# A polysketch attention with an FFN behind it: the order of its instructions from a table of priorities, more PSUM banks for the first FFN product, and batch 1's kv kept on chip

## The chip, the cores and the metric

The kernel runs on one core of a Trainium2 chip. The metric is device time in microseconds (us), the median of the runs; lower is better. One core has TensorE (PE: matmuls; PEld: the loading of their weights), VectorE (DVE), ScalarE (ACT), GpSimd (POOL) and SyncE (SP, which only issues DMAs here). Each engine works through its own list of instructions in order, and waits on semaphores for the others.

## The reference

```python
def _attn_ref(q, k, v, S1, S2):              # 4 batches, 4 heads, 1088 tokens, 32 wide
    ...
    def phi(x):
        a = np.einsum('rd,bhsd->bhsr', S1, x)    # r = 8
        b = np.einsum('rd,bhsd->bhsr', S2, x)
        return np.einsum('bhsi,bhsj->bhsij', a, b).reshape(*x.shape[:-1], r * r)
    q_p, k_p = (phi(q), phi(k))
    kv = np.einsum('bhsf,bhsd->bhfd', k_p, v)
    z = np.sum(k_p, axis=2)
    num = np.einsum('bhsf,bhfd->bhsd', q_p, kv)
    den = np.einsum('bhsf,bhf->bhs', q_p, z)[..., None] + 1e-06
    return (num / den).astype(np.float32)

def _moe_ref(x, w_in, w_out):                # 4352 x 128, 128 x 2048, 2048 x 128
    h = x @ w_in
    g = h - np.tanh(h)
    return (g @ w_out).astype(np.float32)
```

The attention's result, its heads side by side, is the FFN's x.

## The kernel before, in words

**Attention, batch by batch.** For each of the four batches k is loaded and transposed by DVE (tile kT, L602), sketched by PE (L620, "ksk"), transposed back (abk, L634, "kab"), and its outer products are formed on DVE (w, L680, three pieces); PE multiplies them with v into kv (L692). A small gram product (L652, L643) with two ACT copies (gm, L661; sc, L668) gives the denominator's weights. kv then has to be brought into the form that the numerator reads, the tile kvb (`kv_tail`, L716). For batch 0 this is done on chip: a copy kvd (L728), two PE transposes (L735), a copy kvb (L738). For batches 1 to 3 DVE transposes into kvd (L719), SP stores it to a scratch tensor kvx in memory (L721, called kvs) and loads it four times from there into kvb (L723). On q's side DVE transposes (qT, L611), PE sketches (L756, "qsk"), DVE transposes back (abc, L762), divides (m, den, rd, ap: L774 to L782), and forms outer products (qp, L800) and their transposes (qpT, L805), three pairs for a whole batch. PE's numerator (L818, "num") needs kvb and qpT, fills four PSUM banks and is copied to xT in two halves (L390) by ACT or DVE. The next batch's sketch needs those banks, so it waits for the copies.

**FFN, in ten groups of columns.** `GCOLS` (L19) cuts the 4352 token columns into groups of 256, 384, 448, six of 512, and 192. A group has 16 first products, h = w_in's block times xT (L927), 16 tanhs by ACT (th, L931) and 18 second products that add up in one bank (16 with th, L942, and two correction products of xT with w_in w_out, split in two bf16 parts wch and wcl, L946); then DVE transposes the bank (ot, L951) and SP stores it (L961). Groups 0 to 2 are batch 0's columns, 3 and 4 lie in batch 1's, 5 begins there and needs batch 2, 6 lies in batch 2's, and 7 to 9 need batch 3.

**PSUM** has eight banks. Before, the h tiles of groups 0 to 6 turn through banks 0, 1 and 2, one bank to a tanh; the second products use bank 3; attention has banks 4 to 7. From group `PAIRS` = 7 on an h tile takes two banks, (4, 5), (6, 7) or (0, 1), and one tanh reads both; these groups wait for the end of attention (`att_end`).

**The order** is found when the program is built. Every operation is given engines with a planned duration and a delay, a key (lower goes first), its reads and writes, and pools of buffers to choose from. `schedule` (L158) takes at each step, for every engine, the ready operations that could start within a small window (L35) of the earliest, the one with the lowest key among these, and of the engines' choices the earliest; it gives it a free buffer and moves on. So planned durations and keys decide the order on each engine, and which bank an operation gets; nothing is decided at run time. `sync` (L279) then puts in the semaphore waits. Attention's keys count up in program order from -50000 (batch 0's first part -65000); an FFN operation's key is its group's due time plus its number times a step (L915 to L934); loads on SP go first, each held back until an earlier load has landed (`CAPS`, `more`).

Of the kernel before, what the change touches and what calls it, by code (L numbers as in the profile page):

```python
# [12 lines left out]
FP32 = mybir.dt.float32  # L13
# [12 lines left out]
WKEY = (300.0, 300.0, 1500.0)  # L26
PAIRS = 7
URGENT = (-60500.0, 450.0)
# [65 lines left out]
class _Op:  # L94
    __slots__ = ("engs", "fn", "key", "deps", "users", "nleft", "vals", "eng", "lat", "mode",
                 "t0", "t1", "seq", "known", "waits", "inc", "cnt", "sem", "dma", "name", "filler", "parts")


class _Prog:
    SWITCH = 125.0  # L100

    def __init__(self):
        self.ops = []

    def add(self, engs, fn, r=(), w=(), key=0.0, chain=None, dma=0, name="", after=(), mode=None, parts=1):
# [32 lines left out]
        o.deps.pop(o, None)  # L138
        self.ops.append(o)
        return o  # L140

# [219 lines left out]
def bass_polysketch_attn__then__act_tanh_shrink_kernel(  # L361
# [37 lines left out]
    pair_h = _Pool([(pb[i:i + 2], [bank(i, 2)]) for i in (4, 6, 0)], True)  # L399
    att1 = one(4, 5, 6, 7)  # L400
# [106 lines left out]
    def load_k(key, b, more=None):  # L507
        src = k[b].rearrange("h (t r c) d -> (h t) r (c d)", r=2, c=17)
        if b == 0:
            for e in range(2):  # L510
                op = load(key + e, kvals[b][e].ap, src[:, :, e * 288:(544 if e else 288)], [kvals[b][e]], 128 * (256 if e else 288) * 8, issue=750.0, more=more, wire=950.0 - 80 * e)
            return op
        return load(key, kL[b][:, :], k[b].rearrange("h (t c) d -> (h t) (c d)", c=NC), kvals[b] + (kvals[0] if b == 3 else []), 128 * 1088 * 4, cap=2, more=more, wire=1450.0)

    def load_v(key, b, more=None):
        ops = []
        vs = v[b].rearrange("h (m x) d -> m h (x d)", x=17)
        for e in range(2):
            w_ = 256 if e else 288
            ops.append(load(key + e, vL[b][e * 64:(e + 1) * 64, :, 0:w_], vs[:, :, e * 288:e * 288 + w_], [vvals[b][e]] + (vvals[0] if b == 3 else []), 64 * w_ * 16, cap=1 + (b > 0), issue=630.0, more=more, wire=1150.0 - 80 * e))  # L520
        return ops

    def load_q(key, b, i, more=None):
        a, z, val = qvals[b][i]
        src = q[b].rearrange("h (t c) d -> (h t) (c d)", c=NC)
        return load(key, qL[b][:, a * 32:z * 32], src[:, a * 32:z * 32], [val] + ([x[2] for x in qvals[0]] if b == 3 else []), 128 * (z - a) * 128, cap=1 + (b > 0), more=more, wire=(z - a) * 43.0 + 100)

# [59 lines left out]
    def nk():  # L587
        seq[0] += 1
        return -50000.0 + seq[0] + bias[0]
# [80 lines left out]
    wvs = {}  # L670
    kvx = [nc.dram_tensor(f"kvx{i}", [128, 64], FP32, kind="Internal").ap() for i in range(3)]

# [43 lines left out]
    def kv_tail(b):  # L716
        kvd, kvb = _Val(kvd_p), kvbv[b]
        if b:
            P.add(_vp(64), lambda e, n: e.transpose(kvd.ap[:, 0:64], pv[b].ap[:, 0:64]), r=[pv[b]], w=[kvd], key=nk(), name=f"kvd{b}")  # L719
            kvs = _Val()  # L720
            P.add({"sync": (450.0, 0.0)}, lambda e, n: e.dma_start(out=kvx[b - 1], in_=kvd.ap[:, 0:64]), r=[kvd], w=[kvs], key=nk(),  # L721
                  dma=-2300.0, name=f"kvs{b}")
            P.add({"sync": (450.0 * 4, 0.0)}, lambda e, n: [e.dma_start(  # L723
                out=kvb.ap[g * 32:(g + 1) * 32, :, :, :].rearrange("p h x d -> p h (x d)"),
                in_=kvx[b - 1].rearrange("(h f) y -> f h y", h=4)) for g in range(4)],
                r=[kvs], w=[kvb], key=nk(), dma=-3800.0, parts=4, name=f"kvb{b}")
            return
# [60 lines left out]
    def q_piece(b, s0, b0, b1, abc, aq):  # L788
# [24 lines left out]
        def num(e, n):  # L813
# [76 lines left out]
    def weights():  # L890
        for i in range(2):
            tp = _Val(one(4 + 2 * i))
            for j in range(8):
# [20 lines left out]
    def ffn(gi, c0, n_):  # L914
# [8 lines left out]
        for jb in range(NJB):  # L923
            if jb % m == 0:
                hv, th = _Val(pair_h if late else bank_h), _Val(th2_p if late else th_p)
            ths.append((th, jb % m))
            P.add(_pe(n_ / 2.4 + 2.6), lambda e, n, jb=jb, hv=hv: e.matmul(  # L927
                hv.ap[:, jb % m * 512:jb % m * 512 + n_], wic(jb), xt, start=True, stop=True),
                r=[wi[jb // 8]] + xs, w=[hv], key=-60000.0 if gi == 0 and jb < 3 else t0 + jb * step, mode="128x128", name=f"h{gi}.{jb}", after=att_end if late else ())
            if jb % m == m - 1:  # L930
# [110 lines left out]
```

## Time and profile before

| | |
|---|---|
| runs (us) | 112.22, 114.05, 113.49; median 113.49 |
| the profiled execution's own time | 114.35 us |
| its span, first to last instruction | 112.3 us, so 2.05 us lie around it |
| mean granted PE clock | 0.985 of full speed |
| busy: PE, PEld, DVE, ACT, POOL | 99.8, 54.1, 68.3, 78.4, 4.9 us |
| HBM | 9.21 MB read, 2.33 MB written |

A line of the time line reads: start in us, duration in us, engine, source line, operation, output <- input, shapes, how many instructions in a row are merged into it, and in brackets how long the engine sat idle before and for whom. A line of the waits reads: engine, line, whom it waited for, us in total, times, longest. SPq is SP issuing DMAs. The page's part 2 cuts the span into 40 slices of 2.8 us; each digit is the busy share in tenths, PEclk the granted clock in tenths.

### The profile page before, as it was taken

Reading aid. Unit: us, or ns where it says so; the run is one execution under the profiler, and the core shown is the slowest. Engines: PE = TensorE matmul, PEld = TensorE weight load, DVE = VectorE, ACT = ScalarE, POOL = GpSimd, SP = SyncE. Lnnn points to the kernel's source line nnn. Section 1 sums busy time; section 2 is a strip of 40 time slices with the busy share of each in tenths; the row PEclk is TensorE's granted clock in tenths of the full one; section 3 lists DMA queues with packets and bytes.
Section 4 is the critical chain, followed back from the end, with each engine's and each line's share of the span. In section 5 each row is a group of like instructions: output and inputs, shape, how many; then the busy total and the mean of one; then the engine's idle time right before and its main releaser. Section 6 shows DMA issues by size and latency. Waiting matters only on the chain.

```text
span 112.3 us, 3312 instructions
## 1 busy us (share of the span) xinstructions
PE 99.8 (89%) x1421; PEld 54.1 (48%) x1430; DVE 68.3 (61%) x107; ACT 78.4 (70%) x160; POOL 4.9 (4%) x25
## 2 busy tenths in 40 slices
PE   5899969999999927999999999999999999999920
PEld 6746736564564503244633344644444455455800
DVE  4469769999999990099999699998220020200210
ACT  2100747788669851395698687689799999999910
POOL 5250300000000000000000000000000000000000
PEclk9999999999999998599999999999999999999999
DMA  1999798154762397535803400025003214014071
GB/s 19 261 221 198 162 181 317 38 126 90 212 155 88 75 205 166 124 147 85 206 17 67 68 1 0 18 43 97 6 3 58 33 20 73 6 23 70 0 107 24
DMA packets 25087, 10.70 MB, mean 95 GB/s; under 512 B 20977, under 2 KB 23665, under 8 KB 25073
## 3 DMA queue, kind: packets, MB, share of 16 engines
q1 hardware_dynamic: 23792, 9.36, 36.9%
q0 software_dynamic: 576, 1.05, 5.8%
q8 instruction: 11, 0.18, 0.7%
q10 hardware_dynamic: 704, 0.08, 0.5%
q14 instruction: 4, 0.02, 0.1%
HBM read 9.21 MB, written 2.33 MB: 103 GB/s over the span
## 4 chain that ended last, share of the span: by engine, by line
PE 35%; DMA 24%; DVE 15%; ACT 13%; SPq 5%; issue 2%; DVEq 0%
ACT th L931 13%; PE psb L942 13%; PE psb L927 11%; DMA qL<-in_q_dram 9%; DMA vL<-in_v_dram 9%; PE psb L818 5%; SPq L494 4%; DMA kL<-in_k_dram 4%; DVE qp L800 3%; DMA kvb<-kvx 3%; DVE w L680 2%; DVE abc L762 2%; PE psb L620 2%; DVE ot L951 1%; PE psb L692 1%
## 5 line engine op out<-in xcount | busy, mean ns | idle before, releaser
L931 ACT ACTIVATE th<-psb 128x512 bf16<-128x512 f32 (+4 forms) x136 | 69.7, 631 | 11.3 <-PE psb L927 6.9
L927 PE MATMUL psb<-xT,wi 128*128 128x512 bf16 (+4 forms) x154 | 50.3, 362 | 1.3 <-issue 0.4
L942 PE MATMUL psb<-th,wo 128*128 128x512 bf16 (+4 forms) x157 | 47.4, 353 | 1.1 <-issue 1.0
L927 PEld LDWEIGHTS psb<-xT,wi 128*128 128x128 bf16 x160 | 22.0, 145 | 23.6 <-ACT th L931 12.5
L942 PEld LDWEIGHTS psb<-th,wo 128*128 128x128 bf16 x160 | 15.2, 102 | 12.3 <-ACT th L931 4.3
L951 DVE STREAM_TRANSPOSE ot<-psb 128x512 f32<-128x512 f32 (+4 forms) x10 | 6.3, 627 | 24.0 <-PE psb L942 24.0
L805 DVE STREAM_TRANSPOSE qpT<-qp 128x768 f32<-128x768 f32 (+1 forms) x13 | 11.8, 909 | 0.3
L800 DVE TENSOR_TENSOR qp<-ap,abc 128x768 f32<-128x768 f32 (+1 forms) x13 | 11.2, 864 | 0.1
L680 DVE TENSOR_TENSOR w<-abk 128x768 f32<-128x768 f32 x12 | 10.8, 950 | 0.1
L818 PE MATMUL psb<-qpT,kvb 32*32 32x288 f32 (+3 forms) x384 | 8.0, 338 | 2.6 <-DMA kvb<-kvx 2.6
L390 ACT CAST xT<-psb 128x192 bf16<-128x192 f32 (+4 forms) x10 | 4.3, 472 | 6.3 <-PE psb L818 6.3
L454 PE MATMUL psb<-zz 128*128 128x134 bf16 (+1 forms) x56 | 7.2, 298 | 1.1 <-DVE zz L453 1.1
L634 DVE STREAM_TRANSPOSE abk<-psb 128x288 f32<-128x288 f32 x8 | 3.3, 457 | 6.8 <-PE psb L620 6.8
L818 PEld LDWEIGHTS psb<-qpT,kvb 32*32 32x32 f32 x384 | 4.5, 103 | 5.3 <-DMA kvb<-kvx 2.9
L602 DVE STREAM_TRANSPOSE kT<-kL 128x576 f32<-128x576 f32 (+1 forms) x8 | 5.5, 714 | 1.9 <-DMA kL<-in_k_dram 1.9
L454 PEld LDWEIGHTS psb<-zz 128*128 128x128 bf16 x56 | 5.4, 129 | 2.1 <-DVE zz L453 1.1
L762 DVE STREAM_TRANSPOSE abc<-psb 128x1152 f32<-128x1152 f32 (+2 forms) x5 | 5.7, 1140 | 0.9 <-PE psb L756 0.8
L611 DVE STREAM_TRANSPOSE qT<-qL 128x1088 f32<-128x1088 f32 (+2 forms) x5 | 5.3, 1059 | 1.5 <-DMA qL<-in_q_dram 1.5
L692 PE MATMUL psb<-w,vL 128*32 128x64 f32 x288 | 5.3, 221 | 0.2 <-DVE w L680 0.2
L692 PEld LDWEIGHTS psb<-w,vL 128*32 128x32 f32 x288 | 4.3, 110 | 1.4 <-DVE abc L762 0.7
L661 ACT COPY gm<-psb 128x32 f32<-128x32 f32 x4 | 0.8, 190 | 5.0 <-PE psb L652 5.0
L620 PE MATMUL psb<-kT,wab 64*32 64x288 f32 x64 | 3.9, 525 | 0.3 <-POOL wab L563 0.3
(51 smaller groups left out, 45.6 us busy)
## 6 DMA issues: line engine op xcount, KB each, us to landing
kL<-in_k_dram SPq DMA_DIRECT2D x3, 544.0 KB, 4.2
qL<-in_q_dram SPq DMA_DIRECT2D x3, 544.0 KB, 5.0
vL<-in_v_dram SPq DMA_DIRECT2D x4, 288.0 KB, 4.0
vL<-in_v_dram SPq DMA_DIRECT2D x4, 256.0 KB, 4.7
out_dram<-ot SPq DMA_DIRECT2D x16, 64.0 KB, 2.0
wi<-in_moe_w_in_dram POOLq DMA_DIRECT2D x2, 256.0 KB, 6.0
wo<-in_moe_w_out_dram POOLq DMA_DIRECT2D x2, 256.0 KB, 4.8
out_dram<-ot SPq DMA_DIRECT2D x8, 56.0 KB, 1.9
```

What stands on the lines that cost most here:

```text
L454: filler = (lambda c: lambda e, n: e.matmul(bank(3)[:, 0:c], zz.ap[:, 0:128], zz.ap[:, 128:128 + c], start=True, stop=True), zop)
L620: i = e.matmul(pk[rh].ap[g * 32:(g + 1) * 32, 0:288], wab.ap[rh * 64:(rh + 1) * 64, :], kT[b].ap.rearrange("p (j g l) -> p g j l", g=4, l= ...
L680: wlast[:] = [P.add(_v(768), lambda e, n: e.tensor_tensor(out=wv.ap.rearrange("p (x i j) -> p x i j", i=8, j=8), in0=abh(0)[:, :, :, None] ...
L692: i = e.matmul(pv[b].ap[h * 32:(h + 1) * 32, 0:64], vL[b][:, h, blk * 32:(blk + 1) * 32], wvs[b, p].ap[:, (bi * 4 + h) * 64:(bi * 4 + h + ...
L762: abcs[b, s0] = P.add(_vp(sn * 4), lambda e, n: e.transpose(abc.ap.rearrange("p k h f -> p h k f")[:, :, 0:s1 - s0, :], psa4[:, :, 0:sn].r ...
L800: P.add(_v(cn * 256), lambda e, n, qp=qp, c0=c0, cn=cn: e.tensor_tensor(out=qp.ap[:, 0:cn * 256].rearrange("p (x i j) -> p x i j", i=8, j= ...
L805: P.add(_v(cn * 256), lambda e, n, qp=qp, o0=o0, cn=cn: e.transpose(qt.ap[:, o0 * 256:(o0 + cn) * 256], qp.ap[:, 0:cn * 256]), r=[qp], w=[ ...
L818: i = e.matmul(pd[h * 32:(h + 1) * 32, g, 0:nb * 32], kvb.ap[g * 32:(g + 1) * 32, h, x, :], qq[g * 32:(g + 1) * 32, 0:nb, h, x, :], start= ...
L927: P.add(_pe(n_ / 2.4 + 2.6), lambda e, n, jb=jb, hv=hv: e.matmul(hv.ap[:, jb % m * 512:jb % m * 512 + n_], wic(jb), xt, start=True, stop=T ...
L931: P.add(_a(n_ * m), lambda e, n, hv=hv, th=th: e.activation(out=th.ap.rearrange("p (u x) -> p u x", u=m)[:, :, 0:n_], in_=hv.ap.rearrange( ...
L942: fn = lambda e, n, x=x, st=st, sp_=sp_: e.matmul(ov.ap[:, 0:n_], wo[x // 4].ap[:, x % 8, :], ths[x][0].ap[:, ths[x][1] * 512:ths[x][1] * ...
L951: P.add(_vp(n_), lambda e, n: e.transpose(ot.ap[:, 0:n_], ov.ap[:, 0:n_]), r=[ov], w=[ot], key=-60000, name=f"ot{gi}")
```

## The change

1. A table `KEYS` of 141 numbers, found offline, is added to the keys of single operations, named by operation and occurrence (h4.2 is the first product 2 of group 4, o7.10 the second product 10 of group 7). Positive goes later, negative earlier.
2. Planned durations are changed: DVE's operations by 10 ns more, the numerator of nine blocks from 960 to 1650 ns, the loads of batch 0's k, v and q longer, the trip kvs from 2300 to 2800 ns.
3. kv of batch 1 is brought into its form on chip, as batch 0's is (`if b > 1`).
4. From group `HG` = 3 on an h tile of one bank may take any of banks 0, 1, 2, 4, 5, 6, 7.
5. `PAIRS` = 6: two-bank tiles and tanhs begin with group 6, and these groups no longer wait for the end of attention (`LATE` = 0). Second products of groups 6 to 9 use banks 3 and 2, as those of 7 to 9 did.
6. Batch 0's second q load waits for the first half of v's load, not the second.

On the engines the instructions are the same, but for batch 1's kv (on ACT two copies more, on PE two transposes more, on DVE one transpose less, on SP five DMAs less), eight two-bank tanhs in place of 16 one-bank ones, batch 2's second x copy on DVE instead of ACT, and the number of the fill matmuls at the start (L454; they only keep PE busy). Their order differs on PE, DVE, ACT and SP. On PE there stand ahead of the numerators of batches 1, 2 and 3: before 48, 71 and 95 first products and 48, 76 and 103 second ones, after the change 47, 78 and 108 and 50, 82 and 118. kv1 stands 23 FFN products ahead of numerator 1. On DVE batch 3's q transpose is moved ahead, to behind m of batch 2, and the first half of its k transpose into batch 2's qp and qpT. Six two-bank tanhs stand ahead of batch 3's x copy on ACT, and 18 with 1024 elements and 8 with 384 behind it. On SP batch 3's v load now stands ahead of batch 2's kvx.

```diff
-PAIRS = 7
+PAIRS = 6
+KEYS = {
...
+    "h4.13#0": 2025.8, "h4.14#0": 2709.9, "h4.15#0": 1904.4, "h4.2#0": 4733.0, "h4.3#0": 5647.9, "h4.4#0": 2705.2, "h4.5#0": 4958.1, "h4.6#0": 4240.5,
...
+}
+HX = (4, 5, 6, 7)
+HG = 3
+WB = (4, 6)
+LATE = 0
+LB = (4, 6, 0)
...
         self.ops.append(o)
+        self.seen[name] = self.seen.get(name, -1) + 1
+        o.uid = f"{name}#{self.seen[name]}"
+        o.key += KEYS.get(o.uid, 0.0)
         return o
...
-    return {"vector": (n / 0.96 + 64.0, 143.0)}
+    return {"vector": (n / 0.96 + 74.0, 143.0)}
...
-    return {"vector": (n / 0.96 + 76.0, 158.0)}
+    return {"vector": (n / 0.96 + 86.0, 158.0)}
...
     bank_h = one(0, 1, 2)
+    bank_hx = one(0, 1, 2, *HX)
...
-    ld_r = load_q(next(lk), 0, 1, [ld_v[1]])
+    ld_r = load_q(next(lk), 0, 1, [ld_v[0]])
...
     def kv_tail(b):
         kvd, kvb = _Val(kvd_p), kvbv[b]
-        if b:
+        if b > 1:
...
             P.add({"sync": (450.0, 0.0)}, lambda e, n: e.dma_start(out=kvx[b - 2], in_=kvd.ap[:, 0:64]), r=[kvd], w=[kvs], key=nk(),
-                  dma=-2300.0, name=f"kvs{b}")
+                  dma=-2800.0, name=f"kvs{b}")
...
-        P.add(_pe(max(nb * 32 / 1.2, 215.0) * 4), num, r=[kvb, qt], w=pn, key=nk(), mode="32x32", name=f"num{b}.{b0}")
+        P.add(_pe(max(nb * 170.0 + 120.0, 860.0)), num, r=[kvb, qt], w=pn, key=nk(), mode="32x32", name=f"num{b}.{b0}")
...
-                hv, th = _Val(pair_h if late else bank_h), _Val(th2_p if late else th_p)
+                hv, th = _Val(pair_h if late else bank_hx if gi >= HG else bank_h), _Val(th2_p if late else th_p)
...
-                r=[wi[jb // 8]] + xs, w=[hv], key=-60000.0 if gi == 0 and jb < 3 else t0 + jb * step, mode="128x128", name=f"h{gi}.{jb}", after=att_end if late else ())
+                r=[wi[jb // 8]] + xs, w=[hv], key=-60000.0 if gi == 0 and jb < 3 else t0 + jb * step, mode="128x128", name=f"h{gi}.{jb}", after=att_end if late and LATE else ())
```

More of the change, by code (lines that the diff above doesn't have):

```diff
@@ L510, in load_k @@
             for e in range(2):
-                op = load(key + e, kvals[b][e].ap, src[:, :, e * 288:(544 if e else 288)], [kvals[b][e]], 128 * (256 if e else 288) * 8, issue=750.0, more=more, wire=950.0 - 80 * e)
+                op = load(key + e, kvals[b][e].ap, src[:, :, e * 288:(544 if e else 288)], [kvals[b][e]], 128 * (256 if e else 288) * 8, issue=750.0, more=more, wire=1320.0 - 450 * e)
             return op
@@ L670, in bass_polysketch_attn__then__act_tanh_shrink_kernel @@
     wvs = {}
-    kvx = [nc.dram_tensor(f"kvx{i}", [128, 64], FP32, kind="Internal").ap() for i in range(3)]
+    kvx = [nc.dram_tensor(f"kvx{i}", [128, 64], FP32, kind="Internal").ap() for i in range(2)]
     def k_outer(b, p):
@@ L891, in weights @@
         for i in range(2):
[L892 removed]
+            tp = _Val(one(WB[i]))
             for j in range(8):
```

13 lines of the change are left out of this document (7 added, 6 removed), and 19 rows, old and new, of the table KEYS.

## The prediction, on record before the changed kernel was run

> **What bounds the kernel now.** I read the page's 40 slices first, then busy time by stretch, then the waits, then the time line around the places that these pointed to.
>
> ```profile
> PE   5899969999999927999999999999999999999920
> DVE  4469769999999990099999699998220020200210
> ACT  2100747788669851395698687689799999999910
> PEclk9999999999999998599999999999999999999999
> ```
>
> TensorE (PE) is nearly full everywhere except in two slices near 40 us; right behind them VectorE (DVE) drops to 0 and the granted clock falls to 5. In the last quarter ScalarE (ACT) is full. By stretch, cut at the numerators of batches 1, 2 and 3 (the matmuls of L818, which read kvb), that is:
>
> ```profile
> 15.91:40.11 24.20, 23.59 (x395) 13.64 (x386) 23.46 (x36) 19.35 (x54) 0.00 (x0) 1.00 0.53 145
> 40.11:42.73 2.62, 0.00 (x1) 0.00 (x1) 1.75 (x2) 0.84 (x2) 0.00 (x0) 1.00 0.95 155
> 42.73:61.38 18.65, 17.98 (x258) 7.99 (x261) 13.70 (x20) 12.38 (x26) 0.00 (x0) 0.91 0.51 118
> 61.38:78.27 16.89, 16.27 (x260) 7.87 (x262) 14.99 (x21) 13.47 (x28) 0.00 (x0) 1.00 0.23 39
> 78.27:107.01 28.74, 28.28 (x202) 14.74 (x204) 3.56 (x5) 27.84 (x44) 0.00 (x0) 1.00 0.19 29
> ```
>
> The columns are PE, PEld, DVE, ACT and POOL busy, then clock, DMA share and GB/s. PE is the bound up to 78.27, ACT behind it, and between lies a hole of 2.62 us with nothing on PE. The waits and the time line give its cause and its echo:
>
> ```profile
> PEld psb L927 <- ACT th L931: 12.5, 43, 0.5
> ...
> DVE abk L634 <- PE psb L620: 6.8, 2, 5.6
> ...
> PEld psb L942 <- ACT th L931: 4.3, 16, 0.3
> ...
> PE psb L818 <- DMA kvb<-kvx: 2.6, 1, 2.6
> ```
>
> ```profile
> 33.42 0.34 SPq L721 DMA_DIRECT2D kvx<-kvd  x1
> 36.77 1.26 SPq L494 DMA_DIRECT2D vL<-in_v_dram  x2
> 38.07 2.02 SPq L723 DMA_DIRECT2D kvb<-kvx  x4
> ...
> 38.44 0.98 DVE L805 STREAM_TRANSPOSE qpT<-qp 128x768 f32<-128x768 f32 x1
> ...
> 39.70 0.41 PE L927 MATMUL psb<-xT,wi 128*128 128x448 bf16 x1
> 42.73 1.86 PE L818 MATMUL psb<-qpT,kvb 32*32 32x288 f32 x64 [2.62 <-DMA kvb<-kvx]
> ...
> 47.44 0.85 DVE L634 STREAM_TRANSPOSE abk<-psb 128x288 f32<-128x288 f32 x2 [5.58 <-PE psb L620]
> ```
>
> Batch 1's kvb goes to memory and back. SyncE (SP) issues the way out at 33.42, then stands before v's next load until 36.77, and issues the way back at 38.07. It lands when numerator 1 starts, 42.73, though DVE had the operand at 39.42 and PE its last work done at 40.11. Then batch 2's sketch, its transposes (abk) and all of DVE's work come late: DVE idles 5.58 us.
>
> **The change, part by part.**
>
> *kv of batch 1 on chip.* Gone are one kvd transpose on DVE and five DMAs of SP (one kvx, four kvb); added are two PE transposes and two copies on ACT, as batch 0 has them:
>
> ```profile
> 11.47 0.37 ACT L390 COPY kvd<-psb 128x256 f32<-128x256 f32 x1 [2.35 <-PE psb L692]
> ...
> 11.90 0.44 PE L735 MATMUL psb<-ident,kvd 128*128 128x128 f32 x2
> ...
> 12.37 0.37 ACT L390 COPY kvb<-psb 128x256 f32<-128x256 f32 x1 [0.53 <-PE psb L735]
> ...
> 63.15 0.38 PE L927 MATMUL psb<-xT,wi 128*128 128x512 bf16 x1 [0.16 <-issue]
> 63.36 0.38 PE L942 MATMUL psb<-th,wo 128*128 128x512 bf16 x1
> 63.58 0.38 PE L927 MATMUL psb<-xT,wi 128*128 128x512 bf16 x1
> ```
>
> That chain is 1.3 us long (11.47 to 12.74). In the new order kv1 stands 23 FFN matmuls (some 4.4 us at 0.19) ahead of numerator 1, so kvb1 is hidden; without that cover it would cost 1.3 us. Numerator 1 now waits for PE alone. New order: 50 second matmuls ("o") and 47 first ones ("h") ahead of it, where 48 and 48 stood: 40.11 + 2 x 0.19 - 0.19 + 0.44 = 40.7 (DVE's 39.42 is earlier). It was 42.73: **2.0 us earlier**.
>
> *The table of priorities: numerator 1 to 2.* The 512-column cadence is (63.58 - 63.15)/2 = 0.215 us. Between numerators 2 and 3 of the old order stand 24 h and 27 o: 51 x 0.215 = 11.0, so of 16.89 us attention's own PE work, switches and waits take 5.9. The new order puts 31 h and 32 o between numerators 1 and 2 (five of them of 448 columns): 63 x 0.215 - 0.1 = 13.4, + 5.9 = 19.3. Numerator 2 at 60.0, where it was 61.38. Other candidates for that place:
>
> ```profile
> 24.82 1.27 DVE L611 STREAM_TRANSPOSE qT<-qL 128x1088 f32<-128x1088 f32 x1
> ...
> 45.97 0.36 SPq L494 DMA_DIRECT2D qL<-in_q_dram  x1
> ...
> 54.95 0.35 SPq L721 DMA_DIRECT2D kvx<-kvd  x1
> ...
> 60.07 0.94 DVE L805 STREAM_TRANSPOSE qpT<-qp 128x768 f32<-128x768 f32 x1
> ...
> 64.71 0.85 DVE L634 STREAM_TRANSPOSE abk<-psb 128x288 f32<-128x288 f32 x2 [1.26 <-PE psb L620]
> ```
>
> ```profile
> qL<-in_q_dram SPq DMA_DIRECT2D x3, 544.0 KB, 5.0
> ```
>
> DVE: abk came 64.71 - 61.38 = 3.3 us after a numerator at full clock, so 44.0; from abk to the end of qpT it took 61.01 - 47.44 = 13.6, and batch 3's q transpose (1.27) and half of its k transpose (0.7) are moved ahead: 59.6, or 0.4 of slack. But that q transpose comes to its place at some 50.1 (abk 0.9, output transpose 0.6, three w 2.7, abc 1.4, m 0.5 behind 44.0), and its load, if issued at 45.97 as before and 5.0 long, lands at 51.0: up to 0.9 us of DVE, 0.5 of it seen by PE. I count 0.3. SP: from issuing kvx to the numerator 61.38 - 54.95 = 6.4 at most. SP now issues batch 3's v load, which waits for the same q load, ahead of kvx2: 51.0 + 1.3 = 52.3, + 6.4 = 58.7, hidden by 1.3 us. If that cover is gone, each us late is a us on PE.
>
> *Numerator 2 to 3.* 30 h and 36 o: 66 x 0.215 + 5.9 = 20.1, so numerator 3 at 80.1, **1.8 us later** than 78.27. DVE needs 60.0 + 3.3 + (78.07 - 64.71 = 13.4) = 76.7 and is not late:
>
> ```profile
> 75.07 4.03 ACT L931 ACTIVATE th<-psb 128x512 bf16<-128x512 f32 x8 [0.39 <-PE psb L927]
> ...
> 77.09 0.98 DVE L805 STREAM_TRANSPOSE qpT<-qp 128x768 f32<-128x768 f32 x1
> ...
> 80.08 0.38 PE L942 MATMUL psb<-th,wo 128*128 128x512 bf16 x1 [0.21 <-issue]
> ...
> 80.44 26.57 ACT L931 ACTIVATE th<-psb 128x512 bf16<-128x512 f32 x41
> ```
>
> ```profile
> 90.80 13.15 ACT th L931 x14
> ```
>
> *The end, and two-bank tanh from group 6.* (The last row is of the chain of waits.) A one-bank tanh takes 4.03/8 = 0.504 us of ACT, a two-bank one 13.15/14 = 0.939: 0.07 saved per pair, 0.55 for group 6's eight. The old order leaves 41 behind numerator 3 (17 one-bank, 16 two-bank, 8 two-bank of 192): 26.57, so the small ones take (26.57 - 8.57 - 15.02)/8 = 0.37. The new order leaves 18 two-bank and 8 small: 16.9 + 3.0 = 19.9, **6.7 less**. But the first of them reads h tiles that PE issues behind the numerator: 80.08 - 78.27 = 1.8, three matmuls 0.65 and some 0.15 after it, 2.6 us after its start, where ACT went on after 80.44 - 78.27 = 2.2: 0.4 back. Numerator to end of span: 112.30 - 78.27 = 34.0, now 34.0 - 6.7 + 0.4 = 27.7. PE's part of it (52 h and 62 o, 34 of them of 192 columns at 0.08: 80 x 0.215 + 2.7 = 19.9 behind the numerator's 1.8) ends 0.8 us ahead of ACT's 2.6 + 19.9, so ACT holds it, but barely. Span 80.1 + 27.7 = 107.8.
>
> *h tiles in attention's banks* (from group 3). No row shows one. It can take away some of the 16.8 us of weight loads held for a tanh; but numerators 2 and 3 must wait for the tanh that reads a bank of theirs. Lower end: 1 us gained; upper: one one-bank tanh at numerator 2 and one two-bank at numerator 3, 1.4 lost. These waits are of the kind that the old order shows at most 0.5 long, so I take 0.5 lost.
>
> *Start.* Batch 0's second q load is asked for at the first v half, and the first q transpose moves between the two abk:
>
> ```profile
> 6.68 0.45 DVE L611 STREAM_TRANSPOSE qT<-qL 128x256 f32<-128x256 f32 x1 [0.83 <-DMA qL<-in_q_dram]
> ...
> 14.11 1.05 DVE L611 STREAM_TRANSPOSE qT<-qL 128x832 f32<-128x832 f32 x1 [0.69 <-DMA qL<-in_q_dram]
> ```
>
> The load can give back at most 0.69; the transpose, no longer in a wait, costs up to 0.45. The DMAs are already near full there, so I take 0, with -0.3 to +0.5. The new cost figures (DVE, loads) are no instructions; they act through the order alone, as do the fill matmuls at the start.
>
> **Sum.** 107.8 + 0.5 for the banks + 0.3 for DVE's late load = 108.6 against 112.30: 3.7 us less. The profiled execution took 114.35 in all, 0.86 over the median of 113.49; I put the difference on the median: 113.49 - 3.7 = 109.8.
>
> The clock enters this sum. The stretch after the hole ran at 0.91: 18.65 x 0.09 = 1.7 us lost, which I count as gone with the hole. The Trainium skill ("TensorE: Matmul & The Clock Gate", section "HAM oscillation — how this bites in real kernels") wants PE free of gaps above some 3.4 us; the gap here was 2.62 and the clock fell all the same, so the trace is stricter than the page. By the page alone such a gap is too short to cost the clock; the drop would then have another cause and could stay, and the sum would be 109.8 + 1.7 = 111.5.
>
> **Rivals.**
> 1. *The new order gives the gain back in PE's waits for banks*: PE in longer runs of h, held for tanhs, and short gaps that drop the clock. For it: PE has no slack left up to numerator 3. Against: ACT is busy only 12.4 of 18.65 and 13.5 of 16.89. One drop costs 1.7, with its waits of 0.5: 109.8 + 2.2 = 112.0, within 2%. The Trainium skill ("TensorE: Matmul & The Clock Gate", section "A second HAM failure mode: psum-queue depth-cycling") says that cycling through PSUM banks makes PE idle in small pieces until the clock swings; the old kernel cycles through three banks with its clock at 1.00, which speaks against it.
> 2. *The round trip only moves to batch 2*: kvx2 behind v's load on SP. It must lose 1.3 us before numerator 2 waits; if it loses 3.3, as kvb1 did between 33.42 and 36.77, 2 us come back: 111.8.
> 3. *Slower*: h, tanh and o are bound to one another in a fixed order, and a tanh that comes late holds all of PE. The two rows of tanh waits sum to 16.8; the planner's cost of a one-bank tanh (L346: 512 x 0.833 + 50 = 477 ns) is under the 504 worked out above, so that they can grow. From 6.0 us more (3.7 + 2.3), that is by a third, between numerators 1 and 3, the change loses over 2%: 116.
> 4. *Better*: those 16.8 us shrink with seven banks instead of three, 1.0 gained in place of the 0.5 and the 0.3 counted, and the start gives 0.3: 109.8 - 2.1 = 107.7.
> 5. *kv1 doesn't get hidden*: its two copies queue behind ACT's tanhs and numerator 1 still comes near 42. Then some 1.4 us of the gain go: 111.2.
>
> **How the numbers follow.** Forecast 0.60 (109.8, alone 108.0 to 111.0), rival 1 0.14, rival 2 0.07, slower 0.08, better 0.07, rival 5 0.04. The range leaves out the slower case and the far ends: 107.6 to 112.2. A measurement of this kernel can tell about 2% from no change: 111.2 to 115.8 counts as the same. Faster: forecast, better and about half of rivals 2 and 5, 0.73; same 0.19; slower 0.08.
>
> **What would show it.** Right: no PE wait on a DMA for kvb at numerator 1, which starts near 40.7; clock 1.00 throughout; DVE's 5.58 before abk down to about 2; numerators 2 and 3 near 60 and 80; from numerator 3 to the end of ACT about 22.5 us without a gap. Wrong: a clock under 0.95 in any stretch, a kvb wait at numerator 2, DVE standing at batch 3's q transpose for its load, PE waits on tanh above 20 us, or ACT gaps behind numerator 3.

## The result, and the profile after

| | before | after |
|---|---|---|
| runs (us) | 112.22 to 114.05, median 113.39 of 4 | 107.91 to 109.82, median 108.7 of 4 |
| profiled execution: span, own time | 112.3, 114.35 | 107.7, 109.82 |
| mean granted PE clock in it | 0.985 | 1.00 |

The ratio is 0.9596, 95% interval [0.948, 0.9712]: faster. Predicted were 109.8, in a range of 107.6 to 112.2. (Ratios compare undisturbed runs, so they differ a little from quotients of the medians; the profiled execution of the changed kernel was the longest of its four.) Lines have moved by 32: h tiles are L959 now, o tiles L974, tanhs L963, the numerator L850, abk L666, qT L643, kT L634.

The same four rows of the page, 40 slices of the changed kernel:

```profile
PE   5989967969999999899999999999999999999940
DVE  4339975979799999699999928989932002020210
ACT  2201166838878898589699985879996999999930
PEclk9999999999999999999999999999999999999999
```

The hole near 40 us is gone, DVE does not fall to 0 behind it, and the clock is full throughout this profile. New is a thinner start: PE's slices 6 to 9 read 6796 where they read 6999. By stretch, cut at numerator 0's first and last part, numerators 1, 2, 3 and the end of the last tanh (columns: PE, PEld, DVE, ACT, POOL busy, clock, DMA share, GB/s):

```profile
0.00:15.68 15.68, 13.22 (x227) 9.75 (x227) 10.23 (x23) 3.39 (x6) 4.90 (x25) 1.00 0.80 168
15.68:27.19 11.51, 9.51 (x218) 6.13 (x216) 8.81 (x15) 8.04 (x25) 0.00 (x0) 1.00 0.44 126
27.19:42.50 15.31, 15.31 (x272) 8.93 (x271) 14.33 (x21) 13.24 (x34) 0.00 (x0) 1.00 0.59 149
42.50:61.57 19.07, 18.32 (x272) 9.76 (x274) 17.71 (x25) 16.11 (x34) 0.00 (x0) 1.00 0.57 129
61.57:81.12 19.55, 18.98 (x275) 9.79 (x277) 14.58 (x21) 16.56 (x29) 0.00 (x0) 1.00 0.16 28
81.12:103.19 22.07, 21.81 (x175) 12.25 (x176) 2.85 (x4) 21.33 (x28) 0.00 (x0) 1.00 0.23 36
103.19:107.72 4.53, 0.39 (x5) 0.11 (x2) 0.38 (x1) 0.00 (x0) 0.00 (x0) 1.00 0.54 79
```

Numerators 1, 2 and 3 start at 42.50, 61.57 and 81.12, the last tanh ends at 103.19. PE is busy through the whole stretch ahead of numerator 1. The waits and the time line of the changed kernel:

```profile
PEld psb L959 <- ACT th L963: 4.4, 16, 0.5
...
PEld psb L974 <- ACT th L963: 3.2, 11, 0.5
DVE kT L634 <- DMA kL<-in_k_dram: 3.0, 2, 2.1
```

```profile
6.29 0.71 DVE L634 STREAM_TRANSPOSE kT<-kL 128x512 f32<-128x512 f32 x1 [0.92 <-DMA kL<-in_k_dram]
...
45.72 0.85 DVE L666 STREAM_TRANSPOSE abk<-psb 128x288 f32<-128x288 f32 x2 [0.96 <-PE psb L652]
...
51.66 1.31 DVE L643 STREAM_TRANSPOSE qT<-qL 128x1088 f32<-128x1088 f32 x1 [0.19 <-DMA qL<-in_q_dram]
...
83.52 19.67 ACT L963 ACTIVATE th<-psb 128x1024 bf16<-128x1024 f32 x26
```

No row of PE's waits names kvb any more; DVE's 5.58 ahead of abk is 0.96; ACT goes on from 83.52 to the last tanh without a gap. PE's weight loads held for a tanh fell from 16.8 to 7.6 us. And the start is late: DVE stood 0.92 for the second half of batch 0's k, where it had stood for nothing, and PE has two new idle times "for issue", the profile's word for a wait whose cause it does not show: 0.86 ahead of numerator 0 and 1.07 at 22.57 (both are taken up in the last section).

**A measure for the stages.** To compare kernels that put different numbers of h and o tiles (340 in all) into a stage, I take 0.215 us off for each tile, as the prediction did, and 0.08 for the last 34 of 192 columns. What is left I call a stage's rest. The body is the time from numerator 0's last part to the end of the last tanh, the start what lies ahead of it, the tail what lies behind. Changed kernel: 39 tiles in the start (before 35), then 58, 63, 66 and 114; body 76.00, rest 15.9. Before: 61, 51, 51 and 142; body 83.19, rest 22.2. The body of the kernel before in one row, then the two kernels side by side (differences are of the unrounded figures):

```profile
23.83:107.02 83.19, 78.76 (x989) 39.45 (x997) 50.01 (x70) 67.84 (x132) 0.00 (x0) 0.98 0.36 77
```

| us, profiled executions | before | after | difference |
|---|---|---|---|
| start less 0.215 x tiles | 16.3 | 18.8 | +2.5 |
| rest to numerator 1 | 5.8 | 2.8 | -2.9 |
| rest, numerator 1 to 2 | 7.7 | 5.5 | -2.2 |
| rest, numerator 2 to 3 | 5.9 | 5.4 | -0.6 |
| rest, numerator 3 to the last tanh | 2.8 | 2.2 | -0.7 |
| tail | 5.2 | 4.5 | -0.7 |

### The profile page after: what moved, and what is told of

The parts are those of the page before. It is cut to its first block, busy times and chain, and to the rows that moved or that the text cites. A ratio compares the mean times of both kernels' runs of the same rounds, so it can differ in the third digit from the quotient of the medians.

```text
span 107.7 us, 3320 instructions
## 1 busy us (share of the span) xinstructions
PE 97.5 (91%) x1431; PEld 56.7 (53%) x1439; DVE 68.9 (64%) x107; ACT 78.7 (73%) x153; POOL 4.9 (5%) x25
## 4 chain that ended last, share of the span: by engine, by line
PE 83%; DMA 4%; ACT 3%; issue 3%; DVE 1%; SPq 1%
PE psb L959 29%; PE psb L974 28%; PE psb L850 7%; PE psb L724 4%; DMA kL<-in_k_dram 4%; PE psb L978 3%; PE psb L486 3%; PE psb L788 2%; PE psb L652 2%; ACT th L963 2%; ACT xT L421 2%; PE psb L927 1%; PE psb L684 1%; PE psb L937 1%; DVE kT L634 1%
## 5 line engine op out<-in xcount | busy, mean ns | idle before, releaser
L963 ACT ACTIVATE th<-psb 128x512 bf16<-128x512 f32 (+4 forms) x128 | 69.8, 647 | 7.2 <-PE psb L959 4.6
L959 PE MATMUL psb<-xT,wi 128*128 128x512 bf16 (+4 forms) x154 | 43.0, 356 | 1.7 <-issue 0.9
L974 PE MATMUL psb<-th,wo 128*128 128x512 bf16 (+4 forms) x158 | 40.7, 347 | 0.3 <-ACT th L963 0.2
L959 PEld LDWEIGHTS psb<-xT,wi 128*128 128x128 bf16 x160 | 21.6, 146 | 16.8 <-ACT th L963 4.4
L974 PEld LDWEIGHTS psb<-th,wo 128*128 128x128 bf16 x160 | 15.0, 100 | 12.7 <-ACT th L963 3.2
L983 DVE STREAM_TRANSPOSE ot<-psb 128x512 f32<-128x512 f32 (+4 forms) x10 | 6.3, 628 | 18.8 <-PE psb L974 18.8
L486 PE MATMUL psb<-zz 128*128 128x134 bf16 (+1 forms) x63 | 8.1, 300 | 1.1 <-DVE zz L485 1.1
L850 PE MATMUL psb<-qpT,kvb 32*32 32x288 f32 (+3 forms) x384 | 7.7, 332 | 0.0
L634 DVE STREAM_TRANSPOSE kT<-kL 128x576 f32<-128x576 f32 (+1 forms) x8 | 5.6, 719 | 3.0 <-DMA kL<-in_k_dram 3.0
L486 PEld LDWEIGHTS psb<-zz 128*128 128x128 bf16 x63 | 6.2, 128 | 1.9 <-DVE zz L485 1.1
L421 ACT CAST xT<-psb 128x192 bf16<-128x192 f32 (+4 forms) x9 | 3.8, 458 | 3.1 <-PE psb L850 3.1
L850 PEld LDWEIGHTS psb<-qpT,kvb 32*32 32x32 f32 x384 | 4.5, 103 | 2.6 <-ACT th L963 0.8
L666 DVE STREAM_TRANSPOSE abk<-psb 128x288 f32<-128x288 f32 x8 | 3.5, 462 | 3.5 <-PE psb L652 3.5
L643 DVE STREAM_TRANSPOSE qT<-qL 128x1088 f32<-128x1088 f32 (+2 forms) x5 | 5.3, 1051 | 0.2 <-DMA qL<-in_q_dram 0.2
L421 DVE CAST xT<-psb 128x512 bf16<-128x512 f32 (+1 forms) x3 | 1.7, 558 | 5.5 <-PE psb L850 5.5
```

The costliest lines, as they stand in the source:

```text
L421: return e.copy(o, i) if name == "scalar" else e.tensor_copy(o, i)
L486: filler = (lambda c: lambda e, n: e.matmul(bank(3)[:, 0:c], zz.ap[:, 0:128], zz.ap[:, 128:128 + c], start=True, stop=True), zop)
L634: P.add(_v(nb * 64), after=wlast, fn=lambda e, n, e_=e_, nb=nb: e.transpose(kT[b].ap.rearrange("p (j u t r) -> p r j u t", u=2, t=32, r=2) ...
L850: i = e.matmul(pd[h * 32:(h + 1) * 32, g, 0:nb * 32], kvb.ap[g * 32:(g + 1) * 32, h, x, :], qq[g * 32:(g + 1) * 32, 0:nb, h, x, :], start= ...
L963: P.add(_a(n_ * m), lambda e, n, hv=hv, th=th: e.activation(out=th.ap.rearrange("p (u x) -> p u x", u=m)[:, :, 0:n_], in_=hv.ap.rearrange( ...
L974: fn = lambda e, n, x=x, st=st, sp_=sp_: e.matmul(ov.ap[:, 0:n_], wo[x // 4].ap[:, x % 8, :], ths[x][0].ap[:, ths[x][1] * 512:ths[x][1] * ...
```

## The experiments

Three series; each kernel is compared with runs of the kernel before on the same chip. Two theories stood at first. A: batch 1's round trip (kvx, kvb) was the loss, so that its removal alone carries the gain. B: the table carries it, by PE's waits on tanhs. A third, C, came later: part of the loss seen in the first profile belonged to that one execution.

**1. The changed kernel again**, no edit.

> The changed kernel once more, beside the others on one chip. Its first profile began late: numerator 0 at 15.7 us where the kernel before had 13.6. If batch 0's earlier q load does that, it starts late again (numerator 0 at 15.2 to 15.9, wch after 23 us). If it was chance in how batch 0's loads landed, it starts at 13.6 to 14.2 and the span is some 1.5 us shorter than 107.7. Time 108 to 109.5 in both cases.

107.97 us (107.73 to 110.92), before 112.61 (110.57 to 116.98, 23 runs); ratio 0.9721 [0.9654, 0.9789]. The gain is there again, nearer 3 than 4%. Its body:

```profile
28.22:104.24 76.02, 74.43 (x988) 40.84 (x995) 49.38 (x69) 67.25 (x123) 0.00 (x0) 1.00 0.37 80
```

The body repeats to 0.02 us; nearly all that differs between the two profiles lies in the start. Numerator 0 began at 16.02, late again, behind a wait of 1.99 "for issue" where the first profile had 0.86, and the clock fell behind that wait (last section).

**2. kv1 alone**: the kernel before with one edit.

```diff
     def kv_tail(b):
-        if b:
+        if b > 1:
```

> The kernel before with one part of the change alone: kv of batch 1 on chip; no table, old costs, banks and pairs. Theory A (the round trip of kvb1 is the whole of the loss): numerator 1 at 40.5 to 41, clock 1.00, all behind it some 4 us earlier, 109.5. Theory B (the new order and banks make the gain, the hole would be filled or would come back elsewhere): not over 1.5 us less, 112.

111.07 us; ratio 0.9953 [0.9899, 1.0007]. The wait on kvb at numerator 1 is gone and the time hardly moves, as theory B had it. Its profile is marred by a wait of 4.1 us for wo's load in the start, so only the body is read:

```profile
28.95:109.16 80.21, 77.70 (x991) 39.85 (x999) 48.73 (x67) 68.46 (x134) 0.00 (x0) 1.00 0.35 78
```

Theory A falls: kv1 on chip alone is worth nothing that this measurement can tell. Its trace shows where the gain goes. Against the second profile of the kernel before (experiment 8) the rest to numerator 1 is 1.4 shorter (3.2 against 4.6), but the next one, to numerator 2, is 0.8 longer (7.0 against 6.2): numerator 2 now waits for its own trip through memory, what rival 2 of the prediction named for the changed kernel.

```profile
62.64 1.28 PE L818 MATMUL psb<-qpT,kvb 32*32 32x288 f32 x44 [0.65 <-DMA kvb<-kvx]
```

**3. No table**: the changed kernel, its keys not added.

```diff
-        o.key += KEYS.get(o.uid, 0.0)
```

> The changed kernel with the table of priorities left empty; kv1 on chip, costs, banks, pairs as changed. Theory A: at most 1 us over the changed kernel, 109 to 109.7. Theory B (the table's order carries it): most of the gain is gone, 111.5 to 113, and PE's waits for tanhs or numerators show it.

111.31 us; ratio 1.0 [0.9943, 1.0056]. The whole gain is gone, with kv1 on chip, seven banks, corrected costs and two-bank tanhs all in place. Body 77.61 (rest 17.3), against 76.00 (15.9):

```profile
26.22:103.83 77.61, 75.94 (x989) 39.29 (x996) 50.47 (x69) 67.00 (x125) 0.00 (x0) 1.00 0.36 80
```

```profile
PEld psb L958 <- ACT th L962: 8.4, 29, 0.6
PEld psb L973 <- ACT th L962: 7.7, 27, 0.7
```

The table is needed, and the waits on tanhs are back at 16.1. That fits theory B, but experiment 7 will part the two. The body explains 1.6 us of the 3.3 between the medians; this profiled execution was the fastest of its 12, 0.8 under its median; where the rest lies is not seen in a profile. Nor does the table carry all that the body gains: without it the body is still 2.9 shorter than in experiment 8's profile of the kernel before (77.61 against 80.52), and yet the ratio is 1.0. In these two profiles the start less its tiles (38 and 35) is 2.0 longer, 18.1 against 16.1, which takes most of that back.

**4. The second q load later**: the changed kernel's order on every engine, the load's wait alone put back.

```diff
     P.schedule(filler)
+    ld_r.deps.pop(ld_v[0])
+    ld_r.deps[ld_v[1]] = False
```

> The changed kernel in its own order on every engine, with one wait altered: batch 0's second q load waits for v's second half again, as before the change. If the early q load holds up w_in's loads and with them numerator 0: numerator 0 near 14, wch near 21, and 1 to 1.5 us less than the changed kernel beside it, 107.3. If the late start is chance or comes of the new order: no difference over 0.5 us, or 0.3 us more by the later q transpose.

107.69 us; ratio 0.9686 [0.9582, 0.979]: 0.3 under experiment 1 in the same series, and the intervals overlap, so that it is not told apart from it. Body 76.01 again. In its profile numerator 0's last part came at 25.61, where the two of the changed kernel have 27.19 and 28.22; that the load's wait did this is not shown, since those two, of one kernel, already differ by 1.0.

**5. kv1 through memory, the rest as changed.**

```diff
-        if b > 1:
+        if b:
```

(with three scratch tensors kvx again, as before)

> The changed kernel with one part undone: batch 1's kv matrix goes through memory again, as before; the table, the seven banks and two-bank tanhs from group 6 stay. The planner makes room by itself (48 h and 54 o tiles and batch 2's first k tile ahead of numerator 1, against 47 and 50). Theory A (the round trip kvx, kvb was the loss in the old order, and its removal carries the gain): PE waits for kvb at numerator 1 again, 2 us or more, the clock may drop behind it, ratio to the kernel before 0.99 to 1.00. Theory B (the table's order of h, tanh and o tiles carries the gain, by halving PE's waits on tanhs from 16.8 us): the waits on tanhs stay under 10 us, numerator 1 comes up to 2 us later but with more tiles done ahead of it, ratio 0.97 to 0.98, at most 0.01 worse than the whole change (0.9596 to 0.9721).

117.5 us (114.11 to 118.72) where the kernel before had 113.33 in this series: slower by some 4%, by the medians as by the fastest runs (114.11 and 109.67); neither forecast had that. (The runs of the kernel before in this second series spread from 109.67 to 115.91, and there is no ratio with an interval for it; so experiments 6 and 7 go by their bodies.) Time line of PE, and the two stretches around numerator 1:

```profile
44.70 0.72 PE L652 MATMUL psb<-kT,wab 64*32 64x288 f32 x16 [1.41 <-DVE kT L634]
46.94 1.74 PE L850 MATMUL psb<-qpT,kvb 32*32 32x288 f32 x51 [1.53 <-DMA kvb<-kvx]
```

```profile
26.40:46.94 20.54, 17.21 (x290) 9.28 (x290) 18.56 (x28) 13.53 (x33) 0.00 (x0) 1.00 0.62 155
46.94:71.06 24.12, 22.43 (x401) 11.58 (x401) 20.84 (x31) 16.64 (x36) 0.00 (x0) 0.93 0.34 75
```

Two holes, 1.41 for batch 2's k and 1.53 for kvb, then a clock drop, and a rest of 23.9 in place of 15.9. So kv1 on chip, worth nothing alone, is worth up to 8 us of body under this table, some 1.7 of it the clock (24.12 x 0.07). The 8 us are of one profile, and the fastest of the six runs took 3.6 less than the profiled one. (The planner moved other work as well, batch 2's sketch ahead of numerator 1 among it, so they are not the round trip's own price either.)

**6. Three banks for one-bank h tiles**, table kept.

```diff
-HG = 3
+HG = 10
```

> The changed kernel with one part undone: h tiles of one-bank groups keep to the three banks they had before; table, kv1 on the chip and two-bank tanhs from group 6 stay (order of tiles nearly the same: 75 h and 80 o ahead of numerator 2, against 78 and 82). If the seven banks are what takes PE's waits on tanhs down (my rival 'better'), these waits come back to 14 us or more and the ratio to the kernel before is 0.99 or above. If the order does it, the waits stay under 10 us and the ratio is 0.965 to 0.98. If attention's tiles had to wait for h tiles in their banks (my rival 1), this kernel is the faster of the two: 0.955 or less.

109.45 us. Body, and waits on tanhs:

```profile
26.43:104.18 77.75, 77.40 (x996) 40.40 (x995) 49.57 (x69) 67.12 (x123) 0.00 (x0) 1.00 0.36 78
```

```profile
PEld psb L959 <- ACT th L963: 6.2, 23, 0.5
...
PEld psb L974 <- ACT th L963: 4.0, 13, 0.5
```

Body 1.75 longer (rest 17.6): the rest to numerator 2 is 6.6 instead of 5.5, that to numerator 3 6.1 instead of 5.4. The banks gain 1.8 us of body; my forecast of 0.5 lost had the wrong sign, and rival 1 falls. The price that I feared is there, but small: in the changed kernel the numerators' weight loads stood 0.8 us in all for tanhs. (The planner also moved 3 h and 2 o tiles behind numerator 2; the rest takes those out, but not what else their move may do.)

**7. Half the table.** First the 114 entries of the feed-forward's steps alone, then the 27 of attention's alone; the first line of the table as it was and as it then stood:

```diff
-    "aq3.0#0": 147067.4, "den2.0#0": 116420.1, "h0.12#0": 7781.7, "h0.13#0": 7233.8, "h0.15#0": 13082.9, "h0.7#0": -4487.0, "h0.8#0": -990.0,
+    "h0.12#0": 7781.7, "h0.13#0": 7233.8, "h0.15#0": 13082.9, "h0.7#0": -4487.0, "h0.8#0": -990.0, "h0.9#0": 2851.5, "h1.10#0": -3300.8,
```

```diff
-    "aq3.0#0": 147067.4, "den2.0#0": 116420.1, "h0.12#0": 7781.7, "h0.13#0": 7233.8, "h0.15#0": 13082.9, "h0.7#0": -4487.0, "h0.8#0": -990.0,
+    "aq3.0#0": 147067.4, "den2.0#0": 116420.1, "kT0.1#0": 133252.5, "kT1.1#0": 121560.4, "kT2.0#0": 93294.3, "kT2.1#0": 150534.9, "kT3.0#0": 136538.2,
```

> The changed kernel with part of the table: the 114 entries of the feed-forward's steps (h, o, tanh, its x transposes and weight copies); the 27 entries of attention's steps are left out. Theory B1 (what counts is that h and o tiles stand far enough from their tanhs): waits of PE on tanhs under 10 us, ratio to the kernel before 0.965 to 0.98. Theory B2 (what counts is attention's own order, which sets where the numerators come and what PE finds to do between): waits 14 us or more, ratio 0.99 or above, as without the table (1.00).

> The changed kernel with the other part of the table: the 27 entries of attention's steps; the 114 of the feed-forward's are left out. Theory B1: waits of PE on tanhs 14 us or more, ratio 0.99 or above. Theory B2: waits under 10 us, ratio 0.965 to 0.98. If both parts are worth about half, both kernels come to 0.98 to 0.99 with waits near 12 us.

110.86 and 109.75 us. The bodies, feed-forward's half and attention's half, and the waits of the latter:

```profile
26.20:104.25 78.05, 77.65 (x997) 40.29 (x996) 50.51 (x69) 67.12 (x125) 0.00 (x0) 1.00 0.36 80
```

```profile
25.35:102.45 77.10, 76.84 (x998) 39.70 (x997) 50.47 (x71) 67.33 (x125) 0.00 (x0) 1.00 0.36 81
```

```profile
PEld psb L943 <- ACT th L947: 8.6, 31, 0.7
PEld psb L958 <- ACT th L947: 5.6, 21, 0.3
...
PE psb L943 <- ACT th L947: 0.3, 1, 0.3
```

Attention's 27 entries alone take the rest from 17.3 to 16.6, half of the table's 1.4; the 114 others alone take it to 17.7, no gain; together 15.9. **And theory B's mechanism falls.** Attention's half keeps 14.2 us of waits on tanhs, 6.6 more than the whole table, and is 0.7 slower in rest. Feed-forward's half lowers them from 16.1 to 12.9 and gains nothing. The third row says why: while weight loads (PEld) stood 14.2 us for tanhs, the matmuls themselves (PE) stood 0.3. A weight load that waits for a tanh lay here mostly beside a running matmul; its sum is no time lost.

**8. The kernel before, profiled again**, no edit.

> The kernel before, unchanged, profiled a second time. In the first profile PE stood 2.62 us for kvb at numerator 1 and the clock was at half for 3.4 us behind it; from the last third of numerator 0 to the end of the last tanh it took 83.2 us. Theory A (the hole is part of the program): again 2 us or more for kvb, a clock drop behind it, and 82.5 to 84 us. Theory C (hole and drop belong to that one execution; the runs of the kernel before spread from 109.7 to 117.0 us): a wait under 1.2 us, no drop behind numerator 1, and 79 to 81 us, which is what kv1 alone would leave to gain (80.2 there).

111.39 us. Stretches as above, and what stood at numerator 1:

```profile
23.58:41.31 17.73, 16.24 (x273) 8.87 (x272) 17.45 (x25) 14.14 (x35) 0.00 (x0) 1.00 0.61 152
41.31:58.48 17.17, 16.50 (x259) 7.85 (x262) 14.03 (x21) 12.38 (x26) 0.00 (x0) 1.00 0.53 128
58.48:75.35 16.87, 16.25 (x259) 7.87 (x261) 14.99 (x21) 13.47 (x28) 0.00 (x0) 1.00 0.23 39
75.35:104.10 28.75, 28.29 (x202) 14.73 (x204) 3.56 (x5) 27.86 (x44) 0.00 (x0) 1.00 0.19 29
```

```profile
41.31 0.91 PE L818 MATMUL psb<-qpT,kvb 32*32 32x288 f32 x33 [1.44 <-DMA kvb<-kvx]
```

The wait is 1.44, not 2.62; no clock drop behind it; body 80.52, not 83.19, rest 19.5. Theory C holds in the body and the clock, though the wait is between the two forecasts: 2.7 us of the body that I had put on the round trip belonged to one execution. The last two stretches are the same to 0.02 us.

**9. Two-bank tanhs from group 7**, else as changed.

```diff
-PAIRS = 6
+PAIRS = 7
```

> The changed kernel with two-bank tanhs from group 7 on, as before the change, and everything else as changed (110 h and 119 o ahead of numerator 3, against 108 and 118). My term for group 6's pairs was 8 x 0.07 = 0.55 us of ACT behind numerator 3. If the term holds: 0.4 to 0.8 us over the changed kernel, 108.4 to 109.0 where that has 107.9 to 108.3, ratio 0.965 to 0.98. If ACT isn't what holds the end (PE ends within 0.8 us of it): the same time as the changed kernel within 0.3 us.

109.5 us; ratio 0.9794 [0.973, 0.9858].

```profile
25.23:101.91 76.68, 74.74 (x988) 40.70 (x995) 49.68 (x69) 67.52 (x131) 0.00 (x0) 1.00 0.36 79
```

Body 0.68 longer, in time not told apart from experiment 1 (the intervals overlap). By size that is the term of 0.55 us for group 6, and 0.53 of it is rest behind numerator 3. That ACT holds the end, from which the term came, is not shown: here ACT did less behind numerator 3 than in the changed kernel (20.48 us against 21.33) and stood 0.31 and 0.43 for h tiles. In the changed kernel the chain of work that ended last runs through PE there, with no tanh in it, while ACT has no gap from 83.52 on: both are full.

**10. The old cost figures**, table kept.

```diff
-    return {"vector": (n / 0.96 + 74.0, 143.0)}
+    return {"vector": (n / 0.96 + 64.0, 143.0)}
...
-        P.add(_pe(max(nb * 170.0 + 120.0, 860.0)), num, r=[kvb, qt], w=pn, key=nk(), mode="32x32", name=f"num{b}.{b0}")
+        P.add(_pe(max(nb * 32 / 1.2, 215.0) * 4), num, r=[kvb, qt], w=pn, key=nk(), mode="32x32", name=f"num{b}.{b0}")
```

(and likewise the five other figures)

> The changed kernel with the planner's old cost figures (DVE, loads, round trip, numerator) and the table kept; kv1 on the chip, seven banks and two-bank tanhs from group 6 stay. Order of tiles by count: 80 h and 90 o ahead of numerator 2 (78 and 82 in the changed kernel), the rest as there. If the corrected figures matter beside the table (entries were found with them): ratio to the kernel before 0.975 to 0.99, that is 1 to 3 us over the changed kernel. If the table alone carries the order: 0.96 to 0.97, at most 0.5 us over it.

113.19 us; ratio 1.0108 [1.0038, 1.0178]: worse than the kernel before. PE at numerator 2, and the stretch ahead of it:

```profile
67.43 1.74 PE L850 MATMUL psb<-qpT,kvb 32*32 32x288 f32 x64 [1.94 <-DVE qpT L837]
70.41 1.06 PE L959 MATMUL psb<-xT,wi 128*128 128x512 bf16 x2 [1.24 <-DVE xT L421]
```

```profile
39.80:67.43 27.63, 24.38 (x425) 12.12 (x429) 25.28 (x37) 18.33 (x40) 0.00 (x0) 1.00 0.38 89
```

With DVE planned too fast, batch 3's q transpose, both k transposes, abk, w and abc are put ahead of the last qp of batch 2; DVE becomes the bound (25.28 of 27.63 us), numerator 2 stands 1.94 for it, and the rest is 23.2. Some 3.5 of that is the clock, 0.81 in the 18.35 us behind this wait; four of the six runs kept theirs at 0.99 or more and still took 112.41 to 113.55. Figures that are "no instructions" and that I costed at nothing decide the whole gain. That this is because the table was found for them is argued; which of the seven does it was not parted.

**11. Numerator 0 ahead of wi's last transposes**: experiment 4's kernel, with three pieces moved in the finished order.

```diff
     ld_r.deps[ld_v[1]] = False
+    late = [f"wit{i}" for i in range(11, 16)]
+    _move(P.order, late, "num0.0")
+    _move(P.order, ["qsk0.2"], "h0.2")
+    _move(P.order, ["wiT1"], "x0.0.0")
```

> The changed kernel with batch 0's second q load asked for at v's second half (as in the experiment before, 107.69) and, in the finished order, the last five transposes of wi put behind numerator 0's first part, the first three h tiles ahead of the q product, and the copy of x ahead of the copy of the transposed wi. In that experiment PE stood 0.84 us in front of those transposes, ahead of numerator 0. If the start is held by that wait: first h tile 0.8 to 1.4 us earlier behind the same wi landing, time 106.6 to 107.2, ratio 0.955 to 0.965. If the start is held by wo's landing (PE stood 0.46 for it at the weight product): h tiles earlier, but the later numerators where they were, time 107.4 to 108.0, ratio 0.965 to 0.975.

109.28 us; ratio 0.9711 [0.9625, 0.9797]: no gain. The ratio lies in the second forecast's range, the time above it. Its time line:

```profile
13.55 0.34 PE L939 MATMUL psb<-identb,wi 128*128 128x128 bf16 x3
15.38 0.84 PE L862 MATMUL psb<-qpT,kvb 32*32 32x64 f32 x64 [1.49 <-issue]
16.16 0.53 PE L939 MATMUL psb<-identb,wi 128*128 128x128 bf16 x5
```

The gap did not go with the transposes: numerator 0, which took their place, has it now. It was never a wait for wi (below). Body 76.01, as in experiments 1 and 4 to 0.01 us. So no version ran that beats the changed kernel by more than the measurement can tell.

## Why the prediction came out right, and which steps failed

The time was right by 1.1 us, on terms that were partly wrong and, by luck, made up for one another: the sum had 3.7 us gained in the profiled execution, and 4.6 (112.3 to 107.7) were measured.

- *kv of batch 1 hidden, numerator 1 earlier.* The wait went, DVE's idle time with it. Counted 2.0 earlier and one tile more, so 2.2 of rest; measured 2.9. But in the second profile of before only 1.8 of this was there to gain (4.6 of rest against 2.8), and alone it brought nothing (experiment 2).
- *Clock, "1.7 us lost, which I count as gone with the hole".* Gone, but not always there: at 1.00 in the second profile. Failed step: I took a wait of 2.62 and its echo as the program's, and carried the difference of 3.7 us over to the median; the second profile has 1.44 and no echo, so 2.7 us of it were that execution's. By the Trainium skill's rule ("TensorE: Matmul & The Clock Gate", section "HAM oscillation — how this bites in real kernels") such a gap is too short to cost the clock, and for that case the prediction had a drop that could stay, 111.5. It did not stay: the four bodies of the changed kernel's order all ran at 1.00.
- *Numerators 1 to 2 and 2 to 3, "attention's own PE work, switches and waits take 5.9".* 19.3 and 20.1 predicted, 19.07 and 19.55 measured: right within 0.6.
- *Banks, "so I take 0.5 lost".* Failed, with the wrong sign: 1.8 gained (experiment 6). The two stretches above show only 0.2 and 0.6 of that, because under the new order three banks would have had rests of 6.6 and 6.1 there, more than the 5.9 I counted. DVE's late load, counted 0.3, is a wait of DVE of 0.19; what PE saw of it is not parted.
- *Two-bank tanhs from group 6:* 0.55 counted, 0.68 measured, but that ACT holds the end is not borne out (experiment 9). From numerator 3 to the last tanh 22.5 counted, 22.07 measured.
- *Start, "I take 0, with -0.3 to +0.5".* Failed: +2.5 in the first profile, +3.5 in experiment 1's (28.22 less 39 tiles is 19.8, against 16.3), +0.9 in experiment 4's (17.2). In the first profile 0.86 and 1.07 stand at the two gaps "for issue" and 0.92 is DVE's wait for k; they meet other waits, so they do not add up. This is also why numerator 1 came at 42.50 and not at 40.7.
- *Tail:* counted as unchanged, 0.7 shorter.
- *Cost figures and table "act through the order alone".* True, but I read the finished order by counting tiles ahead of numerators, and so could not see that the order is worth what it is only with all of its parts: without the table 1.00, with old costs 1.01, with the round trip some 1.04.

Rivals 1 and 2 did not come: in the changed kernel's bodies there is no clock drop and no wait on kvb at numerator 2. A clock under 0.95 in a stretch, one of my signs of being wrong, did come in experiment 1's profile, at 0.61, but in the start and behind a wait that no rival named. Rivals 3 and 4 both took the 16.8 us of waits on tanhs as time, which experiment 7 denies; rival 4's gain from the banks came all the same. Of the 16.8 us 6.9 lay behind numerator 3, where ACT was full anyway, 27.84 of 28.74 us (waits of the kernel before, from there on):

```profile
PEld psb L942 <- ACT th L931: 3.7, 14, 0.3
PEld psb L927 <- ACT th L931: 3.2, 11, 0.5
```

Rival 5 did not come: numerator 1 waits for no copy.

What stays open: how much of the 3.3 us between the medians of experiments 1 and 3 lies in the start, and why the start is longer. Less its tiles it took 16.3 and 16.1 us in the two profiles of the kernel before, and 16.1 to 19.8 in the eleven of the changed kernel and its variants, more scatter than most of the body's differences; the runs without a profile do not show it.

## What to carry to other kernels

An order found by search belongs to everything it was found with: cost figures, buffers, data paths. Judge it whole, and do not expect parts of it to add up; here kv on chip was worth nothing alone, and taking it, the table or the cost figures away cost the whole gain or more. Profile the kernel before twice ahead of putting a price on a hole, and compare stages by what is left after the work put into them, since positions move when tiles do. A sum of weight-load waits is no lost time until some kernel without them is faster.

## What the runs showed of the hardware

**PE stands at fixed counts of its own instructions.** In 11 of the 14 profiles PE stood 0.84 to 1.99 us "for issue" after 222 matmuls (221 in experiment 10), whatever came next: transposes of wi, or numerator 0. In the changed kernel:

```profile
0.00:14.38 14.38, 12.77 (x222) 9.36 (x222) 9.12 (x22) 2.98 (x6) 4.90 (x25) 1.00 0.78 167
```

```profile
15.23 0.53 PE L927 MATMUL psb<-identb,wi 128*128 128x128 bf16 x5 [0.86 <-issue]
...
22.57 0.89 PE L937 MATMUL psb<-wo,wiT 128*128 128x128 bf16 x13 [1.07 <-issue]
```

Counting all records of PE's queue (matmuls, weight loads, semaphore instructions), the trace has 449 ahead of this gap in all eleven. PE's only other idle times of over 0.25 us "for issue" stand behind 705 records (1.07 above, 0.61 in attention's half of experiment 7) and behind 1729 (0.97 in experiment 5): 256 and 1280 further on, whole steps of 256.

Just ahead of each a block of code comes over the DMA engines: one packet on queue 8 between 13.0 and 14.1 in the changed kernel, between 11.1 and 12.2 in the kernel before (queue, packets, MB, share):

```profile
q8 instruction: 1, 0.02, 5.4%
```

```profile
q8 instruction: 1, 0.02, 5.9%
```

At all 14 of these gaps PE went on 1.2 to 1.6 us behind the end of such a packet. In the two profiles of before and in kv1 alone the packet starts at 10.4 to 11.1 instead of 12.0 to 13.1; there PE comes to its 450th record 1.4 to 2.1 us behind the packet's end, and has no such gap. The Trainium skill ("Runtime: NRT & Kernel Launch", section "Instruction fetch mechanics") says that code streams in by blocks of 16 KiB, 256 instructions, on a DMA queue of its own, and that crossing a block's end is mostly hidden. The size agrees (11 packets with 0.18 MB in the whole profile) and so do the steps of 256; the hiding does not, at these places. Loads that fill the DMA engines are not needed for it: they were at 0.89 of their time from 13.0 to 14.1, but at 0.05 during the gap ahead of 22.57. That the block causes the gap is argued from counts and times; no kernel moved it.

**Gaps of 1 to 2 us can drop the clock, but not each time.** Gaps of 1.49 (experiment 11) and 1.99 (experiment 1) at the start were followed by a lower clock, 1.10 (experiment 5) and 1.17 (experiment 6) there too; 1.16 (attention's half of experiment 7) and the 1.44 of experiment 8 were not:

```profile
13.59:15.57 1.98, 0.00 (x1) 0.01 (x1) 0.58 (x2) 0.42 (x1) 0.00 (x0) 1.00 0.86 146
...
18.75:24.86 6.11, 6.06 (x42) 4.20 (x40) 5.02 (x9) 4.76 (x14) 0.00 (x0) 0.61 0.24 85
```

(experiment 1; the second row is the stretch behind numerator 0's first part; in experiment 11 the clock there was 0.55.) The Trainium skill ("TensorE: Matmul & The Clock Gate", section "What's actually happening") says that the activity window runs on by itself and does not start anew with the kernel, so that the point of change varies from run to run. The scatter agrees with that; no run here shows the window itself.

**The body repeats.** Four profiles of the changed kernel's order gave 76.00, 76.02, 76.01 and 76.01 us, while their starts ran from 25.61 to 28.23. The kernel before, with a trip through memory in its body, gave 83.19 and 80.52.

**The tail** is 5.2 us in the three profiles with three round trips and 4.5 to 4.6 in the eleven with two. No run here shows why.
